# Attention with a gated feed-forward block on one core: each value load as two transfers, of 120 and of 8 partitions

## The chip, the cores and the metric

The kernel runs on one core of one Trainium2 chip. The metric is device microseconds of one execution: 909.33 us is the median of three runs of the kernel before (908.33 to 909.49).

## What is computed

The inputs q, k and v have 8 batches, 8 heads, 576 positions and 64 elements a head. Each head is attention under a causal mask: the first four heads of a batch see the last 32 positions, the other four see the positions whose index agrees with their own modulo 32. The heads' outputs, side by side, are 4608 tokens of 512 elements, and go through a normalised, gated feed-forward block of width 1536:

```python
scores = np.where(masks, scale * np.matmul(q, k.transpose(0, 1, 3, 2)), -1e9)
attn = np.exp(scores - scores.max(-1, keepdims=True))
attn_out = np.matmul(attn / (attn.sum(-1, keepdims=True) + 1e-09), v)
x = attn_out.transpose(0, 2, 1, 3).reshape(B * S, H * D)
xn = x / np.sqrt(np.mean(x * x, -1, keepdims=True) + 1e-06) * rms_g
g = xn @ w_gate
out = (g / (1 + np.exp(-g)) * (xn @ w_val)) @ w_out
```

## The kernel before, in words

**Attention** is cut into 32 units, one for a batch and a pair of heads. `load` (line 665) brings the queries (line 679) and keys (line 681) of a unit, `load_v` (line 694) its values (line 702), `unit_s` does the scores and the softmax (products at lines 752 and 761, exponentials at 796 and 810), and `unit_o` the product with the values (lines 848 and 866) and its copies into token tiles (lines 627 and 629).

The values are laid out on the host so that a unit needs one transfer of 128 partitions: 640 float32 numbers a partition for units 0 to 7 (`vz`, 320 KB) and 704 for units 8 to 31 (`vl`, 352 KB). The values of the first four units go into tiles of their own (`bl`). From unit 4 on two buffers (`vt`) take turns, so that the load of a unit can start only after the product of the unit two before. A product reads the values in blocks of 32 partitions, from all four quarters of the 128. The list `PADV` of units with another layout is empty, so that every unit takes the second branch of line 702.

**The feed-forward block** works on chunks of 512 tokens. The first chunk uses plain products (lines 1163, 1173 and 1218), while the weights are read (line 1071, 1 MB each), split into a high and a low part by ScalarE and VectorE (lines 627, 635, 1070 to 1078, 1183), and stored into scratch in DRAM (`wd`, `gvd` and `od`, lines 1083 and 1091). The eight chunks after it are done in pairs (lines 1317 and 1470), with weights that are read back from the scratch (lines 1105 and 1256). The units of the later batches are worked off between these products: units 0 to 3 ahead of everything, 4 to 11 during the first chunk, 12 to 31 during the first three pairs.

**The order of the work** is laid down by a planner. Every step is told to it by `op(engine, cost, ...)`, with what it reads and writes and, for a transfer, its bytes. `Plan.forward` puts all steps of all engines into one list by its costs and a table of due times; the steps' functions are then called in this order. Which place in SBUF a tile gets is read from a table (`PLACE`). Value loads are steps of SP (cost 430, bytes given), so they stand in SP's order between the loads of queries, keys and weights and the stores into the scratch, and SP issues all of them one after the other, each after its waits. One transfer, the keys of unit 0, and two stores at the end are issued by ScalarE. The waits on semaphores are put in by the framework, from what each instruction reads and writes.

Of the kernel before, what the change touches and what calls it, by code (L numbers as in the profile page):

```python
# [25 lines left out]
P = 128  # L26
# [20 lines left out]
EIGHT = 8  # L47
# [37 lines left out]
PADV = ()  # L85
# [159 lines left out]
HALVES = 1  # L245
DLAT = 3500.0
DLAT0 = 2900.0
FETCH0 = 9500.0
FETCH = 5600.0
WCUT = 1  # L250
# [3 lines left out]
REL = {}  # L254
# [27 lines left out]
class Plan:  # L282
# [95 lines left out]
    def forward(self, users, due, hold, due2=None, hold2=None):  # L378
# [20 lines left out]
        held = {}  # L399
        count, bound, there = 4 * FIRST[0] + 2 * FIRST[1], 446, FETCH0  # L400
        table = "exp"
# [12 lines left out]
        while len(out) < n:  # L414
# [42 lines left out]
            if nb:  # L457
                dma = max(dma, s) + nb / DMARATE
                end[i] = dma + (DLAT if s > 60000 else DLAT0)
            else:  # L460
# [12 lines left out]
def attn_moe(ctx: ExitStack, tc: tile.TileContext, qz: bass.AP, qT: bass.AP, kT: bass.AP, vz: bass.AP, vw: bass.AP, vl: bass.AP,  # L473
             wgv: bass.AP, wo: bass.AP, consts: bass.AP, out: bass.AP):
    nc = tc.nc
# [41 lines left out]
    def op(eng, cost, at, fn, reads=(), writes=(), **kw):  # L517
        reads, writes = list(reads), list(writes)
        for k in reads + writes:
            if k[0] == "sl":  # L520
                plan.uses.append((plan.owner[k[1]], len(plan.ops)))
                g = gen[home[k[1]]]
                if g.fresh is True and not g.first:
                    g.fresh = fn
                (writes if g.fresh is fn else reads).append(("bl", g.j))
        plan.op(eng, cost, at, fn, reads=list(dict.fromkeys(reads)), writes=list(dict.fromkeys(writes)), **kw)
# [31 lines left out]
    def wide(slots, dt=None, n=None):  # L558
        g, at = slots[0].g, CH * (slots[0].i - blocks[slots[0].g.j][0])
        v = g.tile()[:, at:at + (n or CH * len(slots))].bitcast(dt or F32)  # L560
        for k, s in enumerate(slots):
            if dt or s.t is None:
                s.t = g.tile()[:, at + CH * k:at + CH * k + CH].bitcast(dt or F32)
        return v

    def keys_of(slots):
        return [s.key for s in slots]
# [126 lines left out]
    def load_v(i):  # L694
        b, p = units[i]
        pro = i < NPRO
        z = homes[i][1] if pro else ()
        n = D * (NBL + 1 if i < EIGHT else NVB) * (1 + (i in PADV))
        va = (lambda: wide(z, None, n)) if pro else (lambda: vts[i % 2][:, 0:n])
        kv = ("v", i if pro else i % 2 + NPRO)  # L700
        op("SP", 430, 0, lambda: nc.sync.dma_start(out=va().rearrange("p (a n) -> p a n", a=2), in_=vw[PADV.index(i)].rearrange("a p n -> p a n")) if i in PADV else
           nc.sync.dma_start(out=va(), in_=vz[i] if i < EIGHT else vl[i - EIGHT]), writes=[kv], bytes_=P * n * 4, run=2560 if i in PADV else 2048, rel=REL.get(i, 0.0), follow="SP" if pro else None)
        vio[i] = va, [kv] + keys_of(z), z

    def banks_of(i):
# [595 lines left out]
    def pair_of_chunks(c):  # L1301
# [80 lines left out]
        def attention_s(at):  # L1382
            for i, a in zip(win, su):
                if a == at:
                    load(i)
                    load_v(i)
                    unit_s(i)
# [179 lines left out]
    for z in LOADS:  # L1567
        if z[0] == "q":
            load(int(z[1]))
        elif z[0] == "v":  # L1570
            load_v(int(z[1]))
        elif z[0] == "c":
            load_consts(int(z[1]))
        else:
            plan.boost = WB
            convert_weights(*queue.pop(0))
            plan.boost = 0.0
# [18 lines left out]
    def begin(u):  # L1596
        for i, a in zip(WIN[0], SAT[0]):
            if a == u:
                load(i)
                load_v(i)  # L1600
                unit_s(i)
# [132 lines left out]
```

## Time and profile before

| what | before |
|---|---|
| median of three runs | 909.33 us (908.33 to 909.49) |
| the profiled execution's own time | 908.33 us |
| its span, from the first to the last instruction | 906.5 us |
| TensorE busy (products) | 891.0 us, 98% |
| VectorE busy | 714.3 us, 79% |
| ScalarE busy | 538.0 us, 59% |
| moved by DMA | 232.83 MB, mean 257 GB/s |
| granted TensorE clock, mean | 0.996 |

In the profile PE is TensorE's products and PEld its loading of weights, DVE is VectorE, ACT ScalarE, POOL GpSimd, and SP the engine that issues the transfers; a q behind a name (SPq, PEldq) stands for the engine's instruction queue. L702 is line 702 of the kernel. `vt<-in_vl_dram` is an instruction that writes a tile `vt` from the input `vl`; buffer numbers are left out. In a row of waits, the engine and line in front waited for what stands behind the arrow; "issue" stands there where the engine waited for nothing that the profile shows. The time "to landing" of a transfer runs from its issue to the last update of its semaphore.

### The profile page before, as it was taken

To read this page: it belongs to the slowest core of one execution; us is meant where nothing else is said; L and a number is where in the kernel's file an instruction comes from. 1 tells how busy PE (TensorE), PEld (TensorE's weight loads), DVE (VectorE), ACT (ScalarE), POOL (GpSimd) and SP (SyncE) were. 2 spreads that over 40 slices of the span, in tenths; PEclk is the share of its full clock that TensorE was granted. 3 is DMA by queue.
4 is the path that set the end of the run, shared out by engine and by line. 5 is a ranking of instruction groups with operands and counts; after the bars stand their busy time and mean duration, and the time that the engine had idled before them with its cause. 6 is when DMAs were issued, how large, how long until landed. Compare 5 with 4: busy or idle time off the path is not lost.

```text
span 906.5 us, 21369 instructions
## 1 busy us (share of the span) xinstructions
PE 891.0 (98%) x8571; PEld 718.5 (79%) x8575; DVE 714.3 (79%) x1207; ACT 538.0 (59%) x1145; POOL 4.1 (0%) x18
## 2 busy tenths in 40 slices
PE   6999999999999999999999999999999999999998
PEld 4777788778878888888887888888888888888886
DVE  4899989999988999866679998555699983356981
ACT  4999878677777783555556764445458333333440
POOL 0000000000000000000000000000000000000000
PEclk9999999999999999999999999999999999999999
DMA  9899997999889758976557569764355796553552
GB/s 356 324 410 411 411 386 250 400 410 390 311 315 327 238 194 287 300 231 190 189 177 231 194 209 363 258 204 145 113 156 186 225 363 236 178 171 93 186 174 82
DMA packets 104612, 232.83 MB, mean 257 GB/s; under 512 B 11328, under 2 KB 13632, under 8 KB 102208
## 3 DMA queue, kind: packets, MB, share of 16 engines
q1 hardware_dynamic: 104080, 230.90, 73.0%
q8 instruction: 68, 1.11, 0.5%
q10 hardware_dynamic: 432, 0.56, 0.2%
q14 instruction: 32, 0.26, 0.1%
HBM read 179.51 MB, written 51.90 MB: 255 GB/s over the span
## 4 chain that ended last, share of the span: by engine, by line
PE 84%; DMA 6%; DVE 4%; ACT 4%; issue 1%; SPq 0%; DVEq 0%
PE a L1317 20%; PE v L1317 13%; PE g L1317 13%; PE a L1470 11%; PE g L1470 7%; PE v L1470 7%; PE pair L752 2%; PE a L1218 2%; PE pair L848 2%; DMA bl<-in_kT_dram 1%; DMA gvd<-bl 1%; DMA vt<-in_vz_dram 1%; PE v L1163 1%; PE g L1163 1%; DMA bl<-in_wgv_dram 1%
## 5 line engine op out<-in xcount | busy, mean ns | idle before, releaser
L1317 PE MATMUL a<-bl,bl 128*128 128x512 f32 x855 | 216.8, 394 | 0.6 <-ACT bl L1325 0.6
L1317 PEld LDWEIGHTS a<-bl,bl 128*128 128x128 f32 x855 | 157.9, 188 | 35.9 <-ACT bl L1325 1.6
L627 ACT CAST bl<-bl 128x512 fp32r<-128x512 f32 (+1 forms) x216 | 132.3, 641 | 79.5 <-DVE bl L1273 22.8
L635 DVE TENSOR_TENSOR bl<-bl,bl 128x512 fp32r<-128x512 f32 x244 | 160.3, 685 | 9.8 <-PE v L1317 3.8
L1317 PE MATMUL v<-bl,bl 128*128 128x512 f32 x573 | 146.6, 391 | 0.4 <-DMA bl<-gvd 0.4
L1317 PE MATMUL g<-bl,bl 128*128 128x512 f32 x570 | 146.0, 391 | 0.0
L1273 DVE TENSOR_TENSOR bl<-bl,bl 128x512 f32<-128x512 f32 x162 | 109.3, 686 | 39.0 <-ACT bl L1334 35.0
L1317 PEld LDWEIGHTS v<-bl,bl 128*128 128x128 f32 x573 | 107.0, 188 | 24.2 <-DMA bl<-gvd 0.8
L1317 PEld LDWEIGHTS g<-bl,bl 128*128 128x128 f32 x570 | 106.5, 188 | 23.3 <-DVE bl L1355 0.8
L1329 DVE TENSOR_TENSOR a<-a,bl 128x512 f32<-128x512 f32 x96 | 66.3, 696 | 69.0 <-PE a L1317 58.8
L1470 PE MATMUL a<-bl,bl 128*128 128x512 f32 x410 | 97.4, 390 | 0.0
L1470 PEld LDWEIGHTS a<-bl,bl 128*128 128x128 f32 x410 | 76.6, 188 | 16.6 <-DVE bl L635 0.4
L1470 PE MATMUL g<-bl,bl 128*128 128x512 f32 x278 | 66.2, 390 | 0.0
L1470 PE MATMUL v<-bl,bl 128*128 128x512 f32 x278 | 65.9, 389 | 0.0
L1334 ACT ACTIVATE bl<-a 128x512 f32<-128x512 f32 x48 | 28.6, 599 | 57.2 <-DVE a L1329 53.3
L1470 PEld LDWEIGHTS g<-bl,bl 128*128 128x128 f32 x278 | 52.1, 188 | 11.0
L1470 PEld LDWEIGHTS v<-bl,bl 128*128 128x128 f32 x278 | 52.2, 188 | 10.8
L1325 ACT COPY bl<-g 128x512 f32<-128x512 f32 x48 | 28.2, 588 | 49.0 <-PE g L1317 44.4
L1325 ACT COPY bl<-v 128x512 f32<-128x512 f32 x48 | 28.2, 587 | 41.3 <-PE v L1317 41.1
L1040 DVE TENSOR_TENSOR bl<-bl,bl 128x512 fp32r<-128x512 f32 (+1 forms) x54 | 45.7, 858 | 0.8 <-ACT bl L627 0.5
L1325 ACT COPY bl<-a 128x512 f32<-128x512 f32 x48 | 28.1, 587 | 20.1 <-PE a L1317 16.6
L629 DVE CAST bl<-bl 128x512 fp32r<-128x512 f32 (+1 forms) x82 | 35.6, 443 | 4.2 <-PE v L1317 1.1
(175 smaller groups left out, 1166.7 us busy)
## 6 DMA issues: line engine op xcount, KB each, us to landing
bl<-gvd SPq DMA_DIRECT2D x288, 256.0 KB, 4.6
bl<-od SPq DMA_DIRECT2D x168, 256.0 KB, 3.8
gvd<-bl SPq DMA_DIRECT2D x12, 1024.0 KB, 8.3
bl<-in_wgv_dram SPq DMA_DIRECT2D x11, 1024.0 KB, 9.8
wd<-bl SPq DMA_DIRECT2D x18, 512.0 KB, 9.8
bl<-wd SPq DMA_DIRECT2D x18, 512.0 KB, 6.5
vt<-in_vl_dram SPq DMA_DIRECT2D x24, 352.0 KB, 5.9
xq<-in_qT_dram SPq DMA_DIRECT2D x28, 288.0 KB, 6.8
```

The lines of the kernel that those rows point to most:

```text
L627: nc.scalar.copy(out=o, in_=i)
L629: nc.vector.tensor_copy(out=o, in_=i)
L635: elementwise(CH, lambda e: both(e).tensor_tensor(out=lo.new(F32R), in0=src(), in1=hi.f32(), op=ALU.subtract), reads + [hi.key], [lo.key])
L752: nc.tensor.matmul(out=pr[at // CH][32 * r:32 * r + 32, at % CH:at % CH + KW], lhsT=tq()[hd, q0:q0 + 32], rhs=tk_()[hd, q0:q0 + KW], start ...
L848: nc.tensor.matmul(out=ends[r % 2][0][n][64 * h:64 * h + 64, at + 32 * lo:at + 32 * hi], lhsT=va()[32 * r:32 * r + 32, D * (6 * n + j):D * ...
L1040: elementwise(len(l) * 256, lambda e, l=l, zs=zs: both(e).tensor_tensor(out=sides(l, 1, F32R), in0=cols(zs), in1=sides(l, 0), op=ALU.subtr ...
L1273: elementwise(CH, lambda e: both(e).tensor_tensor(out=o.new() if fresh else o.t, in0=a.t, in1=b.t, op=how), [a.key, b.key], [o.key])
L1317: nc.tensor.matmul(out=banks[bk], lhsT=w, rhs=xs[k][y].t, start=start and k == 0 and i == 0, stop=stop and k == 1 and i == 2, skip_group_c ...
L1325: op("ACT", act(CH, True), 0, lambda: nc.scalar.copy(out=t.new(), in_=banks[bk]), reads=[bk], writes=[t.key])
L1329: op("DVE", dve(CH), 0, lambda: nc.vector.tensor_tensor(out=banks[bk], in0=banks[bk], in1=t.t, op=ALU.add), reads=[t.key], writes=[bk])
L1334: op("ACT", act(CH, True), 0, lambda: nc.scalar.activation(out=t.new(), in_=banks[bk], func=AF.Silu), reads=[bk], writes=[t.key], tab="silu")
L1470: nc.tensor.matmul(out=banks[bks[j]], lhsT=v, rhs=xs[k][y].t, start=start and k == 0 and i == 0, stop=stop and k == KT - 1 and i == 2, ski ...
```

## The change

`load_v` issues two transfers where it issued one, the first with partitions 0 to 119, the second with partitions 120 to 127, of the same source into the same tile. Both belong to the same step of the planner, which is told the same cost, bytes, reads and writes as before.

```diff
 DLAT0 = 2900.0
+CUT = 120
 FETCH0 = 9500.0
...
         kv = ("v", i if pro else i % 2 + NPRO)
         op("SP", 430, 0, lambda: nc.sync.dma_start(out=va().rearrange("p (a n) -> p a n", a=2), in_=vw[PADV.index(i)].rearrange("a p n -> p a n")) if i in PADV else
-           nc.sync.dma_start(out=va(), in_=vz[i] if i < EIGHT else vl[i - EIGHT]), writes=[kv], bytes_=P * n * 4, run=2560 if i in PADV else 2048, rel=REL.get(i, 0.0), follow="SP" if pro else None)
+           [nc.sync.dma_start(out=va()[r], in_=(vz[i] if i < EIGHT else vl[i - EIGHT])[r]) for r in (slice(0, CUT), slice(CUT, P))], writes=[kv], bytes_=P * n * 4, run=2560 if i in PADV else 2048, rel=REL.get(i, 0.0), follow="SP" if pro else None)
         vio[i] = va, [kv] + keys_of(z), z
```

## Rows read from the trace of the kernel before

**Rows 1.** The page: busy us of each engine, DMA packets, the queue of instructions.

```profile
PE 891.0 (98%) x8571; PEld 718.5 (79%) x8575; DVE 714.3 (79%) x1207; ACT 538.0 (59%) x1145; POOL 4.1 (0%) x18
...
DMA packets 104612, 232.83 MB, mean 257 GB/s; under 512 B 11328, under 2 KB 13632, under 8 KB 102208
...
q8 instruction: 68, 1.11, 0.5%
```

**Rows 2.** Busy time by stretch: each engine (instructions), PE clock, DMA share, GB/s.

```profile
0.00:35.00 35.00, 27.81 (x703) 19.33 (x707) 20.49 (x45) 22.04 (x67) 1.87 (x13) 0.90 0.88 332
35.00:137.00 102.00, 98.28 (x1534) 77.16 (x1529) 92.97 (x176) 92.62 (x240) 0.24 (x1) 1.00 1.02 399
137.00:206.00 69.00, 68.24 (x512) 54.13 (x511) 68.11 (x119) 51.32 (x100) 0.24 (x1) 1.00 0.94 356
206.00:630.00 424.00, 423.74 (x4401) 343.72 (x4400) 342.91 (x564) 257.12 (x536) 1.54 (x2) 1.00 0.75 251
```

**Rows 3.** PE in order of time: start, us, line; idle before it, releaser.

```profile
20.44 0.37 PE L866 MATMUL g<-pT,bl 32*64 32x64 f32 x2 [3.80 <-issue]
...
55.48 0.32 PE L761 MATMUL pair<-xk,xq 64*32 64x64 f32 x8 [1.17 <-issue]
...
109.34 0.18 PE L848 MATMUL v<-pT,vt 32*64 32x32 f32 x1 [1.05 <-issue]
```

**Rows 4.** Waits of PE, 14 to 210 us: us in total, times, longest.

```profile
PE v L1317 <- DMA bl<-gvd: 0.4, 1, 0.4
```

**Rows 5.** The chain that ended last, 54 to 90 us: start, us, what.

```profile
54.99 11.43 DMA vt<-in_vz_dram
...
66.51 8.90 DMA bl<-in_wgv_dram
...
75.42 5.21 DMA gvd<-bl
...
89.37 0.64 PE pair L752 x40
```

**Rows 6.** SP's issues in order of time, 82 to 92.5 us: start, us, line.

```profile
82.22 0.33 SPq L702 DMA_DIRECT2D vt<-in_vl_dram  x1
83.52 1.11 SPq L1091 DMA_DIRECT2D od<-bl  x2
...
92.16 0.51 SPq L702 DMA_DIRECT2D vt<-in_vl_dram  x1
```

**Rows 7.** Waits of SP over the whole span: us in total, times, longest.

```profile
SPq L1091 <- DMA bl<-in_wgv_dram: 8.5, 4, 3.0
...
SPq L702 <- DMA vt<-in_vl_dram: 1.7, 2, 1.2
```

**Rows 8.** Line 702: 35 to 206 us, then after 206: ns min/median/max; landings.

```profile
L702 SPq DMA_DIRECT2D vt<-in_vl_dram x7: 327/333/1207, 82.2 to 198.8; - x7
L702 SPq DMA_DIRECT2D vt<-in_vz_dram x2: 333/432/530, 55.0 to 67.8; - x2
...
DMA to landing us min/median/max: 7.5/9.8/11.4
...
L702 SPq DMA_DIRECT2D vt<-in_vl_dram x17: 327/333/1442, 219.5 to 622.1; - x17
...
DMA to landing us min/median/max: 2.9/5.0/8.0
```

**Rows 9.** DMA issues of the whole span: count, KB each, us to landing.

```profile
bl<-gvd SPq DMA_DIRECT2D x288, 256.0 KB, 4.6
...
vt<-in_vl_dram SPq DMA_DIRECT2D x24, 352.0 KB, 5.9
...
bl<-in_vz_dram SPq DMA_DIRECT2D x4, 320.0 KB, 8.3
vt<-in_vz_dram SPq DMA_DIRECT2D x4, 320.0 KB, 7.9
```

**Rows 10.** First product with values of unit 8 (timeline), and line 1317's wait instructions.

```profile
95.95 0.13 PEld L848 LDWEIGHTS pair<-pT,vt 32*64 32x64 f32 x1 [0.35 <-issue]
...
L1317 PEldq EVENT_SEMAPHORE  x110: 51/51/2394, 160.4 to 841.1; - x110
```

## The prediction

> **What bounds the kernel now.** Read first the busy shares. TensorE (PE) is busy for 98% of the span [rows 1], so time can be lost or won only where it idles. The table of stretches says where that is: 7.2 of the first 35 us, 3.7 between 35 and 137, 0.8 between 137 and 206, and 0.3 in the 424 us after that [rows 2]. After 630 us no value is loaded any more. The granted clock is 1.00 from 35 us on, so no term below needs a correction for it. The same table shows where transfers are tight: the DMA engines are busy for 1.02 and 0.94 of the time between 35 and 206 us, at 399 and 356 GB/s, and for 0.75 up to 630 us. Between 35 and 137 us VectorE and ScalarE are busy for 93 of 102 us too, so a delay there finds little slack.
>
> Next, what PE waits for. Its three longest waits, 3.80, 1.17 and 1.05 us, have "issue" as their releaser: PE waited for nothing that the profile shows, neither for values nor for another load [rows 3]. The longest wait that PE itself puts down to a transfer is 0.4 us [rows 4]. Transfers act on PE only by a detour, which the chain of waits shows: a value load of 11.43 us, whose landing lets a weight load start (8.90 us), whose landing lets a store start, after which VectorE, ScalarE and, at 89.37 us, PE go on [rows 5].
>
> Why the landing of values lets a weight load start is seen in SP's own order. The value load issued at 82.22 us is the first of nine issues; the ninth is the next value load, at 92.16 us, and seven others lie between them in six rows (the one at 83.52 us is two) [rows 6]. SP's waits have line 702 waiting for just such a load, and a store of line 1091 waiting 8.5 us in all for weight loads whose data it doesn't use [rows 7]. A landing of 9.9 us puts the first one's end at 92.1, where the ninth starts. So eight transfers are in flight at most, and a ninth waits for the first.
>
> **The change, part by part.** There are 32 value loads, of 320 KB up to unit 7 and of 352 KB for the 24 others [rows 9]. By their issue times nine lie between 35 and 206 us, 17 later, and so six before [rows 8]. Each becomes a transfer of 120 rows and one of 8. The planner still sees one step with the same bytes, so neither the order nor the places in SBUF can move. Five things are new.
>
> *SP's issues.* 32 more of them at 0.33 us, the median of line 702 (1.44 at most) [rows 8], are 10.6 us of SP's time. While transfers are tight SP waits for landings [rows 7] and the issue hides behind that; without this cover it would be 9 x 0.33 = 3 us. I take 0.
>
> *The load on the engines.* The page counts 11328 packets under 512 bytes [rows 1]. Divided by 16 engines that is 708, the sum of the counts in the view of DMA issues, from 288 [rows 9] down to single ones in 28 rows: each transfer uses all 16 today, with eight of 128 rows on each. No row shows a transfer of 120 or of 8 partitions. At 399 GB/s one of 16 engines moves 25 bytes a ns, and a row of 2816 bytes (352 KB / 128) takes it 0.11 us. Bounds: if the whole small transfer falls on one engine, that one has 8 x 0.11 = 0.88 us more per load; if the engine that is behind the others gets none of the 128 rows, it has 0.88 us less. I take one row more for the slowest engine, 0.11 us, nearest to the even spread of the packet count. For the nine loads of the tight stretch that is 1.0 us, between -7.9 and +7.9. PE sees of it what goes along the chain to 89.37 us: the two value loads at 55.0 and 67.8 us [rows 8], 0.2 us. Later ones meet PE's waits of 0.4 us and less. I take 0.3 us in all.
>
> *The places in flight.* A load now takes two of eight places, so each transfer behind it is issued one landing later, 9.94 / 8 = 1.24 us on the mean of [rows 6]. This costs nothing while data are still queued on the engines: with eight places a value load takes 9.8 us to land there, with seven about 8.6, and the shortest landing after 206 us is 2.9 us [rows 8]. The engines keep working through the queue. I take 0. If that cover is gone: 9 x 1.24 = 11.2 us.
>
> *The landing of the values.* The second part is issued when the next place comes free, behind the load at 82.22 us at 83.52, 1.3 us later [rows 6]. Its user, the product of line 848, starts at 95.95 us [rows 10], 3.9 us after the landing at 92.1. Today no engine's wait names values. In the first 35 us the wait of 3.80 us without a releaser comes after the first values and covers 6 x 0.11 us; after 206 us the DMA engines have a quarter of their time free. I take 0; without the 3.9 us it would be 1.3 us for a load.
>
> *Waits on PE.* PE has two landings to wait for. A separate wait instruction takes 51 ns on its queue; line 1317 has 110 of them [rows 10], most in the stretch in which PE idles for 0.3 of 424 us. At most 32 x 0.051 = 1.6 us; I take 0.
>
> **The sum.** 0 + 0.3 + 0 + 0 + 0 = 0.3 us. The profiled execution has a span of 906.5 us and a time of 908.33 us, 1.8 us around the span and 1.0 us under the median of the three runs (909.33). So 908.6 us for it, which is **909.6 us** at the median.
>
> **The rivals.** *Fewer bytes in flight, slower.* Place: SP's queue between 35 and 206 us. If the engines run dry because a transfer of 20 or 22 KB (8 of 128 rows) holds one of eight places for a whole landing, every load delays what is behind it by up to 1.24 us. It decides from the point at which what is queued ahead of a new transfer is done in under 2.9 us. Half of the nine loads: 5.6 us, 914.9 us. For it: SP waits for places time and again. Against it: landings of 7.5 to 11.4 us, more than twice the shortest [rows 8]. [...] No row shows a transfer so small. Chance 0.08.
>
> *Rows heaped on one engine, slower.* If the eight rows go to one engine, and that is the last to finish, transfers take 7.9 us longer in the tight stretch. PE would see about a third, because VectorE and ScalarE, which stand between them, are free for 9 of 102 us and take up part: 2.6 us, 911.9 us. For it: nothing shows how 8 rows are spread. Against it: 16 packets for every transfer today. Chance 0.10.
>
> *The slowest engine is relieved, faster.* Instructions come by the same engines: 68 packets on queue q8 take 0.5% of 16 engines' span, 0.005 x 16 x 906.5 / 68 = 1.07 us each [rows 1]. An engine hit by several of them lags and holds up all eight places. If 120 rows leave out just that engine, it saves 0.88 us a load. PE can win back what it idles between 35 and 206 us, 4.5 us, less the two waits without a releaser, 2.2 us: 2.3 us, 907.0 us. For it: SP's waits for landings. Against it: PE hardly waits for transfers, and the relief must fall on the right engine. [...] Chance 0.10.
>
> *Nothing happens.* Both parts end up as one transfer, or all of it is hidden: 909.3 us, inside the forecast's own range.
>
> **How the numbers follow.** The forecast, with the case of nothing, gets 0.72, the others 0.08, 0.10 and 0.10. A measurement of this kernel can tell about 0.2%, 1.8 us, from no change: faster is under 907.5, slower over 911.2. Faster: most of the relief, 0.08. Slower: the places and the larger part of the heaped rows, 0.16. Same: 0.76. The range goes down to 908.2, just under the fastest run before, and up to 912.2 to take in the heaped rows; the places above it (0.08) and the relief below it (0.10) are left out.
>
> **What would show it.** Right: 740 transfers, 64 of them by line 702 at 0.33 us; as many packets over 512 bytes as before, and 740 x 16 = 11840 small ones if every transfer goes on using 16 engines; no engine waiting for values; PE's idle time between 35 and 206 us within 0.5 us of 4.5. [...] The places are right if the DMA share between 35 and 137 us falls below 1.0 and the chain lengthens at value loads. The heaped rows show as value landings beyond 12 us and longer waits of VectorE for stores, the relief as value landings well below 9 us between 35 and 137 us. The forecast fails if PE has a wait of over 1.8 us that the profile of before doesn't have, above all one without a releaser, which no row prices.

## The result, and the profile after

The changed kernel takes 914.16 us (median of four runs, 913.59 to 914.8), the kernel before 908.83 us beside it. The ratio is 1.0051, with a 95% interval of 1.0037 to 1.0066: half a per cent slower, 5.3 us. The forecast was 909.6 us and no difference, with a range up to 912.2 us; both were wrong. The lines of the changed kernel are those of before plus one from line 248 on.

The page of the changed kernel, whose profiled execution took 914.8 us, beside [rows 1]:

```profile
span 913.0 us, 21398 instructions
...
PE 894.6 (98%) x8575; PEld 719.9 (79%) x8575; DVE 714.7 (78%) x1207; ACT 537.6 (59%) x1145; POOL 3.8 (0%) x18
...
DMA packets 104836, 232.83 MB, mean 255 GB/s; under 512 B 11552, under 2 KB 13856, under 8 KB 102432
```

The same bytes, and 224 small packets more: 32 x (15 + 8 - 16). A whole load has 16, one for an engine; the 23 of the two parts fit 120 rows on 15 engines and 8 rows on eight, an estimate from the counts alone. The DMA issues of the whole span show both parts of each load (count, KB each):

```profile
vt<-in_vl_dram SPq DMA_DIRECT2D x24, 330.0 KB
...
bl<-in_vz_dram SPq DMA_DIRECT2D x4, 300.0 KB
vt<-in_vz_dram SPq DMA_DIRECT2D x4, 300.0 KB
...
vt<-in_vl_dram SPq DMA_DIRECT2D x24, 22.0 KB
```

The stretches, with the columns of [rows 2]:

```profile
0.00:35.00 35.00, 27.47 (x632) 18.46 (x633) 19.24 (x44) 18.89 (x64) 1.86 (x13) 0.94 0.96 290
35.00:137.00 102.00, 97.34 (x1584) 75.57 (x1582) 90.49 (x169) 91.02 (x236) 0.37 (x1) 0.99 1.02 374
137.00:206.00 69.00, 66.86 (x505) 52.87 (x504) 65.63 (x116) 52.00 (x100) 0.24 (x1) 1.00 0.99 364
206.00:630.00 424.00, 423.56 (x4332) 343.40 (x4331) 345.54 (x570) 257.46 (x541) 1.04 (x2) 1.00 0.77 257
```

Read the last two columns against each other. In the first 35 us the DMA engines are busier than before (0.96 for 0.88) and move less (290 GB/s for 332); between 35 and 137 us they are as busy (1.02) and move 374 for 399. Each packet takes longer. That is neither of the two ways the prediction thought of: engines that run dry would be less busy, and a few rows more on one engine would leave the packets as they were. The records of single packets say it directly: a row of 2560 bytes of the values took 168 ns on the mean in the first 35 us, 105 before.

Where the delay arises is seen by the same products in both timelines:

```profile
59.57 0.32 PE L762 MATMUL pair<-xk,xq 64*32 64x64 f32 x8 [1.15 <-issue]
...
113.67 0.18 PE L849 MATMUL v<-pT,vt 32*64 32x32 f32 x1 [1.24 <-issue]
...
149.84 1.67 PE L1164 MATMUL v<-bl,bl 128*128 128x512 f32 x6 [1.17 <-DVE bl L1201]
166.92 1.66 PE L1318 MATMUL v<-bl,bl 128*128 128x512 f32 x6 [0.67 <-DMA bl<-gvd]
```

The first two are the products at 55.48 and 109.34 us of [rows 3]: 4.1 and 4.3 us late. The fourth is the product behind [rows 4], at 160.31 us before: 6.6 us late, and so it stays to the end (the span is 6.5 us longer). So the delay arises in two places, 4.1 us before 60 us and 2.3 us between 114 and 167. The wait of 3.80 us at 20.44 us [rows 3] is gone, and several shorter ones stand earlier and later. The others of over 1 us between 10 and 40 us, with the product at 14.40 us for comparison, first before, then after:

```profile
11.31 1.27 PE L761 MATMUL a<-bl 128*64 128x64 f32 x36 [1.26 <-DMA bl<-in_kT_dram]
14.40 1.27 PE L761 MATMUL pair<-bl 128*64 128x64 f32 x36 [0.15 <-DMA bl<-in_kT_dram]
```

```profile
12.43 1.27 PE L762 MATMUL a<-bl 128*64 128x64 f32 x36 [1.75 <-DMA bl<-in_kT_dram]
...
17.04 2.19 PE L762 MATMUL pair<-bl 128*64 128x64 f32 x36 [1.68 <-DMA bl<-in_kT_dram]
...
26.31 1.20 PE L867 MATMUL a<-bl,bl 32*64 32x64 f32 x66 [1.16 <-issue]
32.62 0.61 PE L867 MATMUL pair<-bl,bl 32*64 32x64 f32 x25 [1.57 <-issue]
```

The first two of either kernel wait for loads of keys, which nobody changed: 1.26 and 0.15 us before, 1.75 and 1.68 after.

Waits are only part of the delay. TensorE idles 18.4 us (913.0 - 894.6) where it idled 15.5 (906.5 - 891.0), 2.9 us more; the other 3.6 us of the longer span are busy time, in which nearly the same number of products took longer. Part of that is the granted clock. Here are the stretches at its lower level (0.50), after, and then before:

```profile
17.00:20.40 3.40, 3.36 (x84) 3.27 (x85) 1.28 (x4) 0.38 (x1) 0.43 (x2) 0.50 1.00 257
...
34.00:37.50 3.50, 3.50 (x72) 2.04 (x74) 1.15 (x3) 2.29 (x3) 0.00 (x0) 0.51 1.01 412
```

```profile
18.60:25.40 6.80, 4.96 (x100) 3.80 (x103) 2.57 (x5) 3.61 (x8) 0.00 (x0) 0.50 1.04 406
```

Both kernels have about 7 us of it. Before, it begins inside the wait of 3.80 us, so that TensorE is busy in only 4.96 us of it. After, it comes behind the waits of 1.75 and 1.68 us and again behind those of 1.16 and 1.57 us, and TensorE is busy in nearly all of it. The 36 products above show the price: 1.27 us at 14.40 us before, 2.19 us at 17.04 us after. How much of the 3.6 us this makes in all isn't shown.

The chain that ended last, in the first 37 us (start, us, what):

```profile
2.09 5.43 DMA bl<-in_kT_dram
...
7.54 10.28 DMA bl<-in_vz_dram
...
17.84 0.35 SPq L680
...
18.23 8.41 DMA xq<-in_qT_dram
...
26.70 9.83 DMA bl<-in_wo_dram
...
36.64 1.13 ACT bl L1071
```

It runs through transfers and SP's issues alone: the large part of unit 1's values, whose landing lets SP issue queries, whose landing lets it issue weights, for which ScalarE waits with their split (line 1071, 1070 before). The load of weights ahead of that one (`wgv`) is issued 7 us later than before, at 25.82 us instead of 18.58. First before, then after (start, us, line):

```profile
7.45 0.80 SPq L1071 DMA_DIRECT2D bl<-in_wgv_dram  x2
...
18.58 0.84 SPq L1071 DMA_DIRECT2D bl<-in_wgv_dram  x1
```

```profile
9.42 3.24 SPq L1072 DMA_DIRECT2D bl<-in_wgv_dram  x2
...
25.82 0.38 SPq L1072 DMA_DIRECT2D bl<-in_wgv_dram  x1
```

ScalarE's waits up to 210 us (us in total, times, longest), before and after, give the measure used below:

```profile
ACT bl L1070 <- DMA bl<-in_wgv_dram: 2.0, 1, 2.0
```

```profile
ACT bl L1071 <- DMA bl<-in_wgv_dram: 14.1, 6, 4.5
```

The second delay comes by the same path, a late load of weights for which ScalarE waits. The chain before the wait at 149.84 us:

```profile
113.76 9.77 DMA xq<-in_qT_dram
...
126.89 12.16 DMA bl<-in_wgv_dram
...
139.07 1.16 ACT bl L1071
```

These are loads of queries and weights; what the slower rows of the values add to them isn't shown apart.

### The profile page after: what moved, and what is told of

Read it like the earlier page. It is cut to its first block, busy times and chain, and to the rows that moved or that the text cites. A ratio compares the mean times of both kernels' runs of the same rounds, so it can differ in the third digit from the quotient of the medians.

```text
span 913.0 us, 21398 instructions
## 1 busy us (share of the span) xinstructions
PE 894.6 (98%) x8575; PEld 719.9 (79%) x8575; DVE 714.7 (78%) x1207; ACT 537.6 (59%) x1145; POOL 3.8 (0%) x18
## 4 chain that ended last, share of the span: by engine, by line
PE 80%; ACT 9%; DMA 8%; DVE 2%; issue 1%; SPq 1%; DVEq 0%; ACTq 0%
PE a L1318 21%; PE v L1318 14%; PE g L1318 14%; PE a L1471 11%; PE g L1471 7%; PE v L1471 7%; PE pair L753 2%; DMA xq<-in_qT_dram 2%; PE pair L849 1%; DMA bl<-in_wgv_dram 1%; PE a L1219 1%; ACT pp L797 1%; ACT pp L811 1%; DMA bl<-in_vz_dram 1%; DMA bl<-in_wo_dram 1%; ACT bl L1071 1%
```

## The experiments

Three causes were open: the second transfer itself (its issue, its place among the eight in flight), the uneven shares of the engines, and the way in which 120 rows are spread. In the expectations A stands for the spread over the rows (which rows are written by which engine), B for a cost of smaller transfers as such, whichever rows they hold, and C, D, E and F for what they say there. Which rows collide by A, and which don't, was the author's assumption each time; no run shows which engine writes which row. Each edit is one to the tuple of parts in the changed line 703, unless shown otherwise.

**Two transfers of all 128 rows, by columns.**

```diff
-va()[r] ... for r in (slice(0, CUT), slice(CUT, P))
+va()[:, r] ... for r in (slice(0, n // 2), slice(n // 2, n))
```

> Each value load as two transfers of all 128 partitions, split by columns into two halves. Theory A (the way the rows lie on the engines and the partitions: engines that write certain partitions at the same time slow each other down; in the changed kernel value packets last 168 ns on the mean in place of 105 in the first 35 us): the spread of a 128-partition transfer is back, so 909 to 910 us. Theory B (places: every load holds two of the eight transfers in flight): same places as in the change, so about 914 us. Theory C (uneven shares: 120 and 8 rows give some engines nine rows and others none): even shares, so 909 to 910 us.

909.73 us against 909.7, ratio 0.9999 (0.999 to 1.0009). ScalarE's wait for weights is back:

```profile
ACT bl L1071 <- DMA bl<-in_wgv_dram: 2.1, 1, 2.1
```

A second transfer, its issue and its place cost nothing. SP does issue the weights of 18.58 us 2.2 us later, at 20.82, but nobody notices.

**Three cuts by rows**: at 64; in the middle (0 to 31, 32 to 95, 96 to 127); the same three sizes with the 64 rows first.

```diff
-for r in (slice(0, CUT), slice(CUT, P))
+for r in (slice(0, 64), slice(64, P))
...
+for r in (slice(0, 32), slice(32, 96), slice(96, P))
...
+for r in (slice(0, 64), slice(64, 96), slice(96, P))
```

> Each value load as two transfers of 64 partitions, 0 to 63 and 64 to 127. All rows can be shared evenly over 16 engines, four and four. Theory A: both halves collide as the 120 rows do, each load takes about 1.64 us of the engines in place of 0.82, as in the change, so about 914 us. Theory B: 914 us. Theory C: 909 to 910 us. [...]

> Each value load as three transfers: partitions 0 to 31, 32 to 95, 96 to 127. Same sizes, number of transfers and shares as the next kernel; only the place of the block of 64 differs. Theory A: the block of 64 costs its plain 0.41 us, the blocks of 32 twice theirs (0.41 each in place of 0.21), 1.23 us a load in place of 0.82. The change cost 5.3 us for 15 loads at 0.83 us more, 0.43 us for each us of the engines: 15 x 0.41 x 0.43 = 2.6 us more, 911.5 us. Theory B: two places more than before, about 919 us, as the next kernel. Theory C: 909 to 910 us, as the next kernel. [...]

> Each value load as three transfers: partitions 0 to 63, 64 to 95, 96 to 127. Theory A: all three collide, 1.64 us a load, 914 us, some 2.5 us more than the kernel with the block of 64 in the middle. Theory B: about 919 us, as that kernel. Theory C: 909 to 910 us, as that kernel. [...]

916.14 us, ratio 1.0071 (1.0055 to 1.0086); 920.22, 1.0107 (1.009 to 1.0124); 919.79, 1.0111 (1.0097 to 1.0125). The cut at 64 puts both parts on all 16 engines, four rows each (11840 small packets, 32 x 16 more than before), and still loses more than the change, so uneven shares aren't needed for the loss. The last two, which were to tell A from B, came out alike, against A. Yet the steps between landings on the engine that lands first (from the semaphores' updates) differed for the first three units: 0.56 to 0.59 us for 64 rows in the middle, 0.78 to 0.86 for rows 0 to 63, where a whole load takes 0.82. Part of both losses goes with a lower granted clock of TensorE: eight of these ten executions have a mean of 0.991 to 0.994, those of the kernel before 0.994 to 0.999. The two others, of the cut in the middle at 0.996 and 0.998, took 917.6 and 917.5 us.

**The control for three transfers**: 128 rows in three column parts.

```diff
-va()[r] ... for r in (slice(0, CUT), slice(CUT, P))
+va()[:, r] ... for r in (slice(0, 256), slice(256, 512), slice(512, n))
```

> The values of a unit in three transfers of 128 rows each, by columns (256, 256, and 128 or 192). The control for the two cuts in three, which cost 10 to 11 us. If the third transfer and its place in flight cost nothing, as the second did: 908.5 to 911 us, and the cuts in three pay for their rows alone. If the third place costs (the 11 us of those two are more than the 7 us of the cut at 64 by one more place): 913 to 916 us. Packets of 1024 bytes are smaller, so a little of a loss could also be theirs: steps on the first engine of up to 0.35 us for 256 columns, where their share of 0.82 us is 0.33.

913.43 us against 909.01, ratio 1.004 (1.0025 to 1.0054). So a third transfer isn't free where the second was. SP issues the weights of 18.58 us still later, and ScalarE waits (start, us, line; then its wait up to 210 us):

```profile
23.50 0.38 SPq L1072 DMA_DIRECT2D bl<-in_wgv_dram  x1
```

```profile
ACT bl L1071 <- DMA bl<-in_wgv_dram: 7.7, 3, 5.5
```

About 4 of the 10 us of the two cuts in three are this. Some of the 4 are the smaller packets: the three parts of a load in the first 35 us step by about 0.97 us together, where a whole load takes 0.82. How the rest divides wasn't tried.

**A whole load and a small transfer behind it**: 8 rows of 512 columns into a spare tile.

```diff
-(va()[r], ...) for r in (slice(0, CUT), slice(CUT, P))
+(va(), ...), (spare[8 * (i % 16):8 * (i % 16) + 8, :], ...[CUT:P, 0:CH])
```

> Each load of values whole, in 128 rows, and behind it a transfer of 8 rows of 512 columns into a spare tile that nobody reads; nothing of the computation is changed. If the second, small transfer is what costs (its place, its issue, its landing): 912 to 915 us. If the first part of 120 rows is what costs: 908.5 to 911 us, with the first engine's step for the whole load back at 0.82 us and 0.2 to 0.3 us for the small one; the 8 extra packets of about 0.1 us on each of 8 engines are then lost among the rest.

910.32 us, ratio 1.0011 (1.0001 to 1.0021). An extra small transfer costs about a fifth of the loss, so most of it must come with the large part no longer being a whole load.

**The change for units 0 to 5 alone, and for the others alone.**

```diff
+for r in ((slice(0, CUT), slice(CUT, P)) if i < 6 else (slice(0, P),))
...
+for r in ((slice(0, CUT), slice(CUT, P)) if i >= 6 else (slice(0, P),))
```

> The change for units 0 to 5 alone, whose values are loaded in the first 35 us; the other 26 whole. The trace of the changed kernel is 4.1 us behind that of before at 56 us and stays so to 112 us, and 6.5 us at the end. If the loss arises where the lag grows: 3 to 4.5 us over the kernel before, 912 to 913.5 us. If the stretch with 1.0 of the DMA engines busy (35 to 206 us) makes the loss: under 1 us, 909 to 910 us.

> The change for units 6 to 31 alone, the counterpart of the run with units 0 to 5 alone, which gave 4.9 of the change's 5.3 us. If the first 35 us make the loss: 909 to 910.5 us. If the nine loads between 35 and 206 us cost as much by themselves and the two losses overlap: 911.5 to 913.5 us.

913.93 us against 909.01, ratio 1.0046 (1.0033 to 1.006), and 912.59 against 908.92, 1.0034 (1.0022 to 1.0046). The first 35 us alone make almost the whole loss, but the later loads alone make 3.7 us too: the second was expected to be small, and isn't. The two losses overlap, 4.9 + 3.7 for 5.3 together; why wasn't tried.

**Other cuts in two**: at 126 (nine rows on each of 14 engines), at 117 (nine on 13) and at 104 (eight on 13). The counts of small packets, 11328, 11584 and 11616, fit these engines.

```diff
-for r in (slice(0, CUT), slice(CUT, P))
+for r in (slice(0, 126), slice(126, P))
...
+for r in (slice(0, 117), slice(117, P))
...
+for r in (slice(0, 104), slice(104, P))
```

> The change with the cut at row 126 in place of 120: two transfers again, of 126 and of 2 rows, two places in flight. With runs of equal length for each engine (11552 small packets bore that out for 120 and 8) 126 rows are 14 engines with nine rows each. [...] Theory B (each row of a transfer that isn't all 128 costs more): packets of 160 ns or more, 913 to 917 us. Theory D (engines left out cost): worse than the cut at 120, 914 to 918 us.

> The cut at row 117: 13 engines with nine rows each, and 11 rows on 11 engines. [...] By B 913 to 917 us, and by D, with three engines without a row of the large part, 915 to 919 us.

> The cut at row 104: 13 engines too, with eight rows each, and 24 rows on 12 engines, two each. [...] If only the number of engines counts, the same time as the cut at 117.

912.99 us, ratio 1.0049 (1.0034 to 1.0064); 915.04, 1.0061 (1.0047 to 1.0075); 916.33, 1.0074 (1.006 to 1.0087). Nine rows an engine lose as eight do, with packets of 155 and 149 ns for the 168 of the change and the 146 at 104. The author had taken A to mean that nine rows an engine (at 126 and 117) escape the loss, with 911.5 us at most, and eight don't; no run shows the pattern that this assumed, and the times speak against it.

**The rows' cost by itself**: the kernel before, with series of transfers behind its last store, eight in flight, 2048 bytes a row.

```diff
         for fn in plan.order():
             fn()
+        rows = {"a": (0, 128), "b": (0, 120), "c": (0, 126), "d": (0, 117), "e": (0, 104), "f": (0, 64), "g": (32, 96), "h": (64, 128), "s": (120, 128)}
+        into = [t[:, a:a + CH] for t, a in ((xq[0], 0), (xq[0], CH), (xq[1], 0), (xq[1], CH), (vts[0], 0), (vts[1], 0), (xk[0], 0), (xk[1], 0))]
+        series = "".join(z * (24 // len(z)) for z in ("a", "b", "c", "d", "e", "f", "g", "h", "bs", "ag", "ab", "a"))
+        for j, z in enumerate(series):
+            r = slice(*rows[z])
+            nc.sync.dma_start(out=into[j % 8][r], in_=vl[j % 24][r, 0:CH])
```

> The kernel before with nothing of it changed, and behind its last store series of 24 transfers each, of 2048 bytes a row, into tiles that are free by then, eight in flight: of all 128 rows, of 0 to 119, 0 to 125, 0 to 116, 0 to 103, 0 to 63, 32 to 95, 64 to 127, then 120 and 8 rows in turn, all 128 and 32 to 95 in turn, all 128 and 0 to 119 in turn, and all 128 once more. It measures the rows' cost by itself, without a kernel around it; the time of the whole is then 909 us and some 250 us more, and only the packets and landings at its end are read. A 2048 byte packet of the loads of all 128 rows takes 84 ns in the kernel. [...] Theory B (every shape but 128 rows pays, whichever rows they are): 130 to 170 ns for 32 to 95 just as for 0 to 63. Theory E (what costs is that transfers of different spreads overlap): 84 to 95 ns for every series of one shape, and more only in the three mixed ones.

Series of one shape, whole, 120, 126, 117 and 104 rows (columns of [rows 2]):

```profile
906.00:919.00 13.00, 0.00 (x0) 0.00 (x0) 0.00 (x0) 0.00 (x0) 0.00 (x0) 0.54 1.02 373
923.00:938.00 15.00, 0.00 (x0) 0.00 (x0) 0.00 (x0) 0.00 (x0) 0.00 (x0) 0.50 1.00 289
942.00:961.00 19.00, 0.00 (x0) 0.00 (x0) 0.00 (x0) 0.00 (x0) 0.00 (x0) 0.50 0.94 260
965.00:983.00 18.00, 0.00 (x0) 0.00 (x0) 0.00 (x0) 0.00 (x0) 0.00 (x0) 0.50 0.87 258
987.00:1001.00 14.00, 0.00 (x0) 0.00 (x0) 0.00 (x0) 0.00 (x0) 0.00 (x0) 0.50 0.86 297
```

Whole loads move 373 GB/s at 1.02, 120 rows 289 at 1.00: even with no kernel around it a busy engine moves less (a packet takes 109 ns in place of 86, with 126 and 117 rows 115 and 108; with 104 rows alone it takes 84, which stays open). The three series of 64 rows ran at one transfer per 0.64 us with the engines idle in between, bound by the issue, and tell nothing. In turn with whole loads, 32 to 95 had a median of 84 ns and 120 rows a mean of 118. So the next run put each cut in turn with whole loads.

```diff
+... for z in ("a", "af", "ag", "ah", "ab", "ac", "ad", "ae", "ag", "af", "ah", "a"))
```

> As the series before, but every cut in turn with whole loads of 128 rows, so that the engines stay busy (series of 64 rows alone ran at one transfer per 0.64 us whichever rows they were, with the engines idle in between): 128 with 0 to 63, with 32 to 95, with 64 to 127, with 120, 126, 117 and 104, then the three of 64 rows again in another order. Seen so far: 84 ns a packet with 32 to 95 (one in ten over it), 118 with 120. [...] Theory B (all shapes but 128 rows pay): the three of 64 rows alike, within 5 ns and 0.03 us a step. Theory F (runs of more than four rows on an engine cost, whichever they are): all three of 64 rows at 84 ns, the cuts at 120, 126, 117 and 104 at 110 to 125.

Here are, in order, whole loads; whole with 0 to 63; with 32 to 95; with 64 to 127; with 120 rows; then again with 32 to 95, 0 to 63 and 64 to 127:

```profile
907.00:919.00 12.00, 0.00 (x0) 0.00 (x0) 0.00 (x0) 0.00 (x0) 0.00 (x0) 0.50 1.03 374
923.00:937.00 14.00, 0.00 (x0) 0.00 (x0) 0.00 (x0) 0.00 (x0) 0.00 (x0) 0.50 1.07 261
941.00:953.00 12.00, 0.00 (x0) 0.00 (x0) 0.00 (x0) 0.00 (x0) 0.00 (x0) 0.50 0.98 310
957.00:970.00 13.00, 0.00 (x0) 0.00 (x0) 0.00 (x0) 0.00 (x0) 0.00 (x0) 0.50 1.06 252
974.00:993.00 19.00, 0.00 (x0) 0.00 (x0) 0.00 (x0) 0.00 (x0) 0.00 (x0) 0.50 1.04 238
...
1064.00:1076.00 12.00, 0.00 (x0) 0.00 (x0) 0.00 (x0) 0.00 (x0) 0.00 (x0) 0.50 0.96 318
1080.00:1094.00 14.00, 0.00 (x0) 0.00 (x0) 0.00 (x0) 0.00 (x0) 0.00 (x0) 0.50 1.06 244
1098.00:1112.00 14.00, 0.00 (x0) 0.00 (x0) 0.00 (x0) 0.00 (x0) 0.00 (x0) 0.50 1.07 261
```

The three cuts of 64 rows have the same bytes, packets and engines, and differ in their position alone. With rows 32 to 95 the median packet takes 84 ns and about nine in ten no longer, both times, and a few long ones bring the mean to 97 to 100; with rows 0 to 63 the mean is 134 and 141 ns, with 64 to 127 138 and 133. (The 310 and 318 GB/s with 32 to 95 are under those of whole loads alone because SP then issues two transfers of 0.64 us for each 192 rows and hardly waits for landings.) B falls, F can't be the whole cause, and what is left is A in a plain form: the position of the rows counts. Rows 0 to 63 also get twice the writes of the others in that series. Such an uneven load can't be all of it: 120 rows, in turn with whole loads, lie almost evenly and moved least, 238 GB/s. Why the position counts isn't shown: no view shows which engine writes which row, nor whether engines hold each other up. Two things stay open besides: 104 rows alone, whose packets took no longer than those of whole loads (84 ns for 86), and the side that is held up, since each transfer takes the same rows of the array in DRAM as it writes, so that the runs don't tell reading from writing.

**The same in the kernel**: values whole, and an extra transfer of 64 rows behind the loads of units 0 to 2 and 6 to 31, once of rows 0 to 63, once of 32 to 95.

```diff
+(va(), ...), ((vts[i] if i < 2 else spare)[slice(0, 64), 0:CH], ...[slice(0, 64), 0:CH]) [:1 if 2 < i < 6 else 2]
...
+(va(), ...), ((vts[i] if i < 2 else spare)[slice(32, 96), 0:CH], ...[slice(32, 96), 0:CH]) [:1 if 2 < i < 6 else 2]
```

> Values whole, as before, and behind the loads of units 0 to 2 and 6 to 31 one more transfer of 64 rows, 0 to 63, of 2048 bytes each into tiles that nobody reads then. Its pair takes rows 32 to 95; bytes, packets, places and order are the same. In the mixed series a pair of a whole load and rows 0 to 63 took 1.50 to 1.60 us, with rows 32 to 95 1.16 to 1.28, 0.3 to 0.4 us less. 12 of the 29 extra transfers are issued before 206 us. Theory A: the extra rows cost 4 packets of 84 ns on each engine, 0.34 us, and the held-up packets 0.34 more, 8 us in all before 206 us, of which PE sees about 0.43 (5.3 us for 12.5 in the changed kernel), 3.5 us: 911.5 to 914.5 us, values of 2560 bytes in the first 35 us above 112 ns a packet. Theory B: the same time as the pair within 0.7 us.

> As its pair, with rows 32 to 95 for the extra transfers. Theory A: 0.34 us for each of the 12 on the engines, 4 us, of which PE sees 1.7: 909.5 to 912 us, and 1 to 3 us under the pair. Theory B: as the pair within 0.7 us.

914.14 us, ratio 1.0052 (1.0038 to 1.0066), and 909.53 us, ratio 1.0005 (0.9996 to 1.0014), against 909.49. Reading 3.8 MB more (29 x 64 x 2048 bytes) into the middle rows costs nothing that can be told; into the lower rows it costs as much as the change. The clock alone isn't the reason: executions at the same mean clock of 0.994 took 913.5 to 915.4 us with the lower rows, 910.8 and 911.2 with the middle ones. The stretch from 35 to 137 us, and ScalarE's wait for weights up to 210 us, low rows first:

```profile
35.00:137.00 102.00, 95.62 (x1494) 74.36 (x1492) 89.89 (x169) 89.19 (x231) 0.24 (x1) 0.97 1.01 380
```

```profile
ACT bl L1072 <- DMA bl<-in_wgv_dram: 7.5, 3, 3.3
```

```profile
35.00:137.00 102.00, 97.46 (x1568) 76.51 (x1557) 92.13 (x173) 90.75 (x238) 0.24 (x1) 0.98 1.03 395
```

```profile
ACT bl L1072 <- DMA bl<-in_wgv_dram: 3.0, 2, 2.3
```

The cuts in three differ as A has it in their packets (140 ns for the middle, 160 for the low one) and in ScalarE's waits, but not in their times. The two parts of 32 rows and the third transfer, which both have, may hide the difference; that isn't shown. A cut in two with other rows together (0 to 31 with 64 to 95, then the rest) has no measurement, so that a split by rows without the loss stays unshown.

All runs together. Packets are mean ns of the values' rows from the packet records, of 2560 bytes in the first 35 us and of 2816 between 35 and 137; "wait" is ScalarE's wait up to 210 us for loads of weights (rows for wgv and wo added), in us; the ratio is that of the times. For units 0 to 5 alone only the times are used; the profiled execution of units 6 to 31 was its fastest, 909.25 us.

```
                          2560 B  2816 B   wait   ratio
before                      105     116     2.0     -
the change, 120 and 8       168     143    15.3   1.0051
columns, two                  -       -     2.1   0.9999
columns, three                -       -     8.0   1.004
64 and 64                   169     130     8.1   1.0071
126 and 2                   155     122     6.0   1.0049
117 and 11                  149     129     8.8   1.0061
104 and 24                  146     138    15.5   1.0074
middle, three               140     118     8.0   1.0107
low, three                  160     124    18.7   1.0111
units 6 to 31               106     129     6.3   1.0034
whole and 8 rows            113     113     1.9   1.0011
whole and 0 to 63           114     122     7.5   1.0052
whole and 32 to 95          107     116     3.0   1.0005
```

Runs that lose 0.1% or nothing have waits up to 3 us, all others 6 and more; the 6.3 us of units 6 to 31 belong to an execution that lost almost nothing. The size of the wait doesn't give the size of the loss, which depends on where in the chain it falls.

## Why the prediction was wrong, point by point

*What bounds the kernel.* Right in the main: TensorE loses time only before 206 us, mostly by the detour over SP's order, and hardly by waiting for values. After the change too the longest wait for values that the trace names is 2.0 us, once, of TensorE's weight loading (ahead of the product at 17.04 us, where TensorE itself names keys). But not by the detour alone: the waits of [rows 4] were read from 14 us on, and the 1.26 us for keys at 11.31 us, the second longest wait of all, was overlooked. After the change two such waits take 3.4 us. And that no term needs a correction for the clock doesn't hold after the change: a stretch at a granted clock of 0.50 lies behind new waits, from 34.0 to 37.5 us.

*SP's issues*, 0. Held: the cut by columns has as many of them and the same time.

*The places in flight*, 0. Held for two transfers (1.0 times the time of before), by the reason given, that the engines work through what is queued. The cover has an end that the prediction didn't look for: with three transfers 4.4 us are lost. The rival of fewer bytes in flight forecast 914.9 us, near the measured time, but by a mechanism that the runs refute: the DMA share didn't fall below 1.0 between 35 and 137 us, and the cut by columns takes as many places and loses nothing.

*The load on the engines*, 0.3 us. **This is the step that failed.** It priced a row by the rate of whole loads, 0.11 us, and asked only how many rows an engine gets. That took for granted that a row costs the same in a part of the rows as in a whole load. Measured by the landings on the engine that lands first, the two parts of units 0, 1 and 3 took 1.36 to 1.41 and 0.28 to 0.29 us where a whole load took 0.82 to 0.83: some 0.83 us more for a load, not 0.11. (The other three of the first 35 us can't be read apart like this; by the mean of all packets, eight rows of 168 ns for 105, it is 0.5 us.) That lies just inside the bound of 0.88 us, which was meant for another case and was put to use only for the tight stretch. Later loads pay less: 143 ns for 116, times eight rows, is 0.2 us. The page's own numbers could have shown only that nothing priced it: no row had a transfer of other than 128 rows, as the prediction said, and it took the row that was nearest.

*The landing of the values*, 0. Failed in the first 35 us: the wait of 3.80 us was to cover 6 x 0.11 us, and had to cover up to 6 x 0.83 = 5.0 us. It did take up some, since it is gone. By 60 us 4.1 us came through, of which 1.0 us is idle time of TensorE (9.9 of the first 64 us, 8.9 of 60 before) and the rest longer busy time. The expectations of the last pair put 12.5 us for all 15 loads against the loss, as if all paid 0.83; 6 x 0.83 + 9 x 0.2 = 7 us is the most that the measurements give.

*Waits on PE*, 0. Held, no such row appeared.

*The rivals.* Rows heaped on one engine named 911.9 us and transfers that take longer, the right sign by the wrong cause: the small packets fit 8 rows on eight engines. An engine without a row of the 120, the condition of the third rival, fits their count too, but isn't needed for the loss, as the cut at 64, on 16 engines, loses more (0.71% for 0.51%). No gain from a relieved engine shows. Of what would show it, the 11840 small packets did not come; they are 11552. The sign of failure named last, one new wait of over 1.8 us, did not come, though the forecast failed: the loss is spread over waits of up to 1.75 us and over busy time. The idle time between 35 and 206 us, 6.8 us (102 - 97.34 + 69 - 66.86) where 4.5 were expected, shows 2.3 us of it.

## What to carry to other kernels

Keep transfers at all 128 partitions, and split a load by columns when it has to be split: two halves by columns cost nothing here, three parts by columns 0.4%, every cut in two by rows 0.5 to 0.7%. Where a part of the rows is wanted, try its position: as an extra transfer, 64 rows from row 32 on were free here (ratio 1.0005), and from row 0 on they cost as much as the change (1.0052). And when a DMA share stays at 1.0, look at the GB/s beside it before calling the engines full: here the same share, 1.02 between 35 and 137 us, moved 374 GB/s where it had moved 399.

## What the runs showed of the hardware that wasn't expected

The busy share of the DMA engines didn't say what they moved: at a share of 1.04 to 1.07 whole loads in turn with other cuts moved 238 to 261 GB/s, whole loads alone 374 at 1.03. Transfers beside a cut took longer too: rows of 2304 bytes of queries and keys, which nobody changed, took 115 ns in place of 101 in the first 35 us.
